# Ten warm products, no zero fill, and the first loads of q and k on one queue

## The chip, the cores and the metric

The kernel runs on one core of a Trainium2 chip. The metric is the device time of one execution in microseconds (us), the median of several. Before the change it is 364.73 us, the median of three runs from 364.7 to 364.95.

The engines that matter here: TensorE (PE in the profile; its weight loads are PEld), which multiplies and transposes; ScalarE (ACT) and VectorE (DVE), which work elementwise and move results out of PSUM; GpSimd (POOL), which here issues most of the loads; SyncE (SP), which issues DMAs. A DMA can be issued from the queues of SP, ACT and POOL.

## The reference

Attention with a squared relu in place of the softmax, and behind it a feed-forward block with the exact gelu:

```python
batch, n_heads, seq, head_dim = (8, 12, 448, 64)
scores = scale * np.matmul(q, k.transpose(0, 1, 3, 2))
attn = np.maximum(scores, 0.0) ** 2 / S
out = np.matmul(attn, v)
x = out.transpose(0, 2, 1, 3).reshape(B * S, H * D)      # 3584 x 768
h = x @ w_in                                             # 3584 x 2048
g = 0.5 * h * (1.0 + erf(h * inv_sqrt2))
return g @ w_out                                         # 3584 x 768
```

q, k, v and the weights come in float32; the products run in bf16.

## The kernel before

The twelve heads of a batch are taken in three groups of four. For a group, q and k are loaded with the rows of the sequence on the partitions and must be transposed, so that head_dim lies on the partitions. In batches 0 and 1 TensorE does that (`add_tq` and `add_tk`, tile `tp`, lines 676, 680, 708 and 715): a transpose is a product with an identity matrix, and a copy by DVE (line 566) brings the result from PSUM into `qT` and `kT`. From batch 2 on, DMA transposes issued by SP do it (line 742). The scores of 64 keys at a time go into PSUM (`ps`, line 819), ACT takes the relu of most of them (`a_sq`, line 831) and DVE of some (line 833), DVE squares them (line 841), and the products with v follow (`pav`, line 881). The feed-forward block is worked in between (`psh`, line 940), and later alone (lines 1092, 1281, 1388).

The order of the work of each engine is written out by hand in the string `ORDER`. A word is an engine's letter (P, A, D, G, S for PE, ACT, DVE, POOL, SP) and the number of an operation; a word with Z is a fill: products of zeros with that many columns in all, on TensorE (`add_fill`, line 1609). Each engine works through its words in order and waits at each one for what it reads and for the buffer that it writes. POOL's identity matrix (`make_ident`, line 1447) is the operation with the highest number; in `ORDER` it stands behind the first five loads that POOL issues.

Ahead of that list the kernel has a head of its own. The first group's first half of q (`q32`) and its k (`k32`) are loaded as float32, k in two parts: `K_CUT` = 4 blocks of 64 rows and then the remaining three. Then a tile of zeros and the identity's ground are set, a gelu on one column brings ACT's table in, and `SPIN` = 11 products of zeros with 512 columns run on TensorE:

```python
spin = banks.take("spin")
for _ in range(SPIN):
    wide = zero[:, :1].to_broadcast([128, NB])
    nc.tensor.matmul(spin[:, 0], zero, wide, start=True, stop=True)
```

The function `early` (line 1480) then casts what has landed: ACT casts q32 (word A10), DVE the first part of k32 (D13), ACT the second (A16). TensorE's first words are the transposes of this q (P11), of the first four blocks of k (P14) and of the other three (P17); DVE's next ones the copies into qT (D12) and kT (D15, D18). The transposes have two PSUM buffers, so P17 waits until D12 has freed one. P29 and P32 are the first scores. All other loads are issued by POOL, at most eight of them under way.

Of the kernel before, what the change touches and what calls it, by code (L numbers as in the profile page):

```python
# [84 lines left out]

COLD_END = 0.0
K_CUT = 4
SPIN = 11


ORDER = """
D13 G0 Z1056 A10 G1 G7 G4 A16 G108 G1469 P11 D12 P14 D15 P17 P29 P32 D18 P38 D39 P19 P21 A30 D20 P35
D22 P27 A33 P62 D31 P77 A36 D40 D28 A63 P59 D34 P44 P25 G2 G3 A78 A60 D37 D45 G111 P121 P65 A66 P71
A72 P47 P74 A75 D79 A48 D122 D64 D67 P23 D73 P50 D24 D26 P68 G107 P41 A51 P98 A69 D76 A99 D61 D52
D70 P53 P123 G5 G115 G112 A42 A43 G8 G116 A54 G6 P95 P86 A96 A87 P80 D46 D124 A81 A82 P89 P92 P119
# [339 lines left out]
def kernel(  # L435
# [9 lines left out]
    nc = tc.nc  # L445
# [25 lines left out]
    k32 = wpool.tile([128, 2, NK * D], F32, tag="t4", name="k32")  # L471
# [36 lines left out]
    def q_view(b, g0, g1, c0, c1):  # L508
        qq = q[b, 4 * g0 : 4 * g1].rearrange("h (p c) d -> p h (c d)", c=NC)
        return qq[:, :, c0 * D : c1 * D]  # L510
# [5 lines left out]
    def kv_view(t, b, g0, g1):  # L516

        return t[b, 4 * g0 : 4 * g1].rearrange("h s d -> (h s d)").rearrange(
            "(x p f) -> p x f", p=128, f=NK * D
        )  # L520
# [915 lines left out]


    first = slice(0, K_CUT * D)
    nc.scalar.dma_start(k32[:, :, first], kv_view(k, 0, 0, 1)[:, :, first])
    nc.sync.dma_start(q32, q_view(0, 0, 1, 0, HC))  # L1440
    rest = slice(K_CUT * D, NK * D)
    nc.scalar.dma_start(k32[:, :, rest], kv_view(k, 0, 0, 1)[:, :, rest])
    zero = const.tile([128, 128], BF16, tag="zero", name="zero")
    V.memset(zero, 0.0)
    V.memset(ident, 0.0)
# [12 lines left out]
# [3 lines that stand above are left out]
# [192 lines left out]
```

## Time and profile before

| what | us |
|---|---|
| median of the runs | 364.73 |
| the profiled execution | 364.86 |
| its span, first to last instruction | 363.1 |
| TensorE busy | 354.5 |
| DVE busy | 296.0 |
| ACT busy | 211.2 |
| POOL busy | 65.4 |

The span is what the profile sees between the first and the last instruction; the execution's time has 1.76 us more. Busy time is the union of an engine's instructions. Matmuls overlap and their ends are modelled, so a busy TensorE need not be at its peak. Times in the rows are in us from the start of the span: a row of the time line is start, duration, engine, line, operation, what is written and read, how many, and in brackets the idle time before it and what ended it. A "q" behind the engine's name is its queue, issuing a DMA. The chain of waits is the sequence of work that ended last, followed back from the last instruction. In answers by stretches a row has the stretch, its length, the busy time and count of PE, PEld, DVE, ACT and POOL, the granted clock of TensorE, the share of the DMA engines and the GB/s.

### The profile page before, as it was taken

What the parts mean: (1) busy time and instruction counts of PE and PEld (TensorE: products, weight loads), DVE (VectorE), ACT (ScalarE), POOL (GpSimd) and SP (SyncE); (2) the same over time, 40 slices, a digit from 0 to 9 for tenths busy, and PEclk for the clock granted to TensorE, in tenths of its full rate; (3) what the DMA queues carried; (4) which work ended last, traced back from release to release, by engine and by line L of the source; (5) the groups of instructions that cost most, each with busy time, mean ns of one, the idle gap of its engine ahead of it and who ended that gap; (6) DMA issues with size and microseconds to landing.
All of it is one profiled execution on the core that took longest, in us unless ns stands there. A gap on an engine that the chain in (4) does not pass through costs nothing.

```text
span 363.1 us, 7640 instructions
## 1 busy us (share of the span) xinstructions
PE 354.5 (98%) x3103; PEld 190.5 (52%) x3103; DVE 296.0 (82%) x497; ACT 211.2 (58%) x354; POOL 65.4 (18%) x102
## 2 busy tenths in 40 slices
PE   8799999999999999999999999999999999999995
PEld 3464544555554555554455555555555555555663
DVE  2999968869999979999979999998966655786552
ACT  3999766446678685777968864625741233662110
POOL 8566174110533051070000000000000000000000
PEclk9999999999999999999999999999999999999999
DMA  9999999999999999999950521000301210302223
GB/s 174 201 202 199 183 175 190 173 197 191 177 183 185 167 196 172 217 146 225 200 113 7 91 68 45 3 0 14 119 0 56 70 49 2 87 2 87 88 88 88
DMA packets 72083, 43.83 MB, mean 121 GB/s; under 512 B 36336, under 2 KB 68720, under 8 KB 72048
## 3 DMA queue, kind: packets, MB, share of 16 engines
q0 software_dynamic: 32032, 22.47, 43.9%
q1 hardware_dynamic: 39120, 20.03, 28.4%
q10 hardware_dynamic: 896, 0.85, 0.7%
q8 instruction: 24, 0.39, 0.5%
q14 instruction: 11, 0.09, 0.1%
HBM read 45.61 MB, written 11.01 MB: 156 GB/s over the span
## 4 chain that ended last, share of the span: by engine, by line
PE 94%; ACT 4%; issue 1%; DVE 1%
PE pso L1281 33%; PE psh L940 21%; PE pb L1092 18%; PE ps L819 9%; PE pav L881 8%; ACT a_sq L831 4%; PE pso L1388 3%; PE spin L1461 1%; ACT xT L568 0%; PE tp L715 0%; PE fill L1615 0%; DVE osb L1315 0%; DVE a_sq L841 0%; DVE qT L566 0%; PE tp L676 0%
## 5 line engine op out<-in xcount | busy, mean ns | idle before, releaser
L831 ACT ACTIVATE a_sq<-ps 128x896 bf16<-128x896 f32 x122 | 107.1, 923 | 29.4 <-PE ps L819 29.0
L841 DVE TENSOR_TENSOR a_sq<-a_sq 128x896 bf16<-128x896 bf16 x169 | 96.5, 614 | 2.0 <-ACT a_sq L831 1.6
L940 PE MATMUL psh<-xT,win_sb 128*128 128x448 bf16 x384 | 77.1, 353 | 0.0
L833 DVE TENSOR_SCALAR a_sq<-ps 128x896 bf16<-128x896 f32 (+1 forms) x47 | 50.5, 1076 | 14.1 <-PE ps L819 13.7
L1281 PEld LDWEIGHTS <-s_sb 128*128 128x128 bf16 x424 | 40.4, 98 | 29.7 <-issue 3.5
L940 PEld LDWEIGHTS <-win_sb 128*128 128x128 bf16 x384 | 35.6, 98 | 38.0 <-issue 7.1
L1123 DVE TENSOR_TENSOR part<-pb,part 128x448 f32<-128x448 f32 x80 | 46.4, 618 | 9.1 <-PE pb L1092 6.2
L819 PE MATMUL ps<-qT,kT 64*64 64x448 bf16 (+1 forms) x700 | 47.9, 350 | 2.2 <-ACT a_sq L831 2.0
L950 ACT ACTIVATE h_sb<-psh 128x448 bf16<-128x448 f32 x64 | 34.5, 548 | 19.0 <-PE psh L940 19.0
L1315 DVE TENSOR_TENSOR osb<-pso,p_sb 128x384 f32<-128x384 f32 x39 | 21.6, 553 | 23.7 <-PE pso L1281 18.2
L1281 PEld LDWEIGHTS <-h_sb 128*128 128x128 bf16 x296 | 28.2, 98 | 21.5 <-issue 3.0
L1281 PE MATMUL pso<-t_sb,s_sb 128*128 128x384 bf16 x208 | 38.1, 326 | 0.0
L1144 ACT ACTIVATE h_sb<-part 128x448 bf16<-128x448 f32 (+1 forms) x48 | 24.5, 537 | 22.8 <-DVE part L1123 22.7
L1281 PE MATMUL pso<-wout_sb,s_sb 128*128 128x384 bf16 (+1 forms) x208 | 37.7, 324 | 0.0
L881 PE MATMUL pav<-a_sq,v_sb 64*64 64x448 bf16 (+1 forms) x700 | 36.0, 342 | 0.8 <-ACT a_sq L831 0.8
L1281 PE MATMUL pso<-wout_sb,h_sb 128*128 128x384 bf16 x192 | 35.2, 326 | 0.0
L819 PEld LDWEIGHTS <-kT 64*64 64x64 bf16 x700 | 18.6, 105 | 25.1 <-issue 17.9
L1092 PEld LDWEIGHTS <-win_sb 128*128 128x128 bf16 x192 | 18.8, 98 | 16.7
L881 PEld LDWEIGHTS <-v_sb 64*64 64x64 bf16 x700 | 20.7, 107 | 12.4 <-issue 1.9
L1092 PE MATMUL pb<-xs,ws 128*128 128x448 bf16 x96 | 21.9, 352 | 0.0
L1092 PE MATMUL pb<-xs,win_sb 128*128 128x448 bf16 x96 | 21.8, 352 | 0.0
L1092 PE MATMUL pb<-xT,win_sb 128*128 128x448 bf16 x96 | 21.7, 352 | 0.0
(73 smaller groups left out, 310.5 us busy)
## 6 DMA issues: line engine op xcount, KB each, us to landing
nk<-in_k_dram POOLq DMA_DIRECT2D x23, 224.0 KB, 8.7
nq<-in_q_dram POOLq DMA_DIRECT2D x23, 224.0 KB, 8.8
v_sb<-in_v_dram POOLq DMA_DIRECT2D x4, 672.0 KB, 9.6
out_dram<-osb SPq DMA_DIRECT2D x7, 336.0 KB, 3.2
v_sb<-in_v_dram POOLq DMA_DIRECT2D x10, 224.0 KB, 8.0
out_dram<-osb SPq DMA_DIRECT2D x7, 288.0 KB, 3.4
out_dram<-osb SPq DMA_DIRECT2D x8, 240.0 KB, 2.8
win_sb<-in_moe_w_in_dram POOLq DMA_DIRECT2D x8, 192.0 KB, 9.4
```

The source lines that it names most:

```text
L819: nc.tensor.matmul(ps[64 * j : 64 * j + 64, e, x * w : x * w + w], kT[r, g, i * 128 + 64 * j : i * 128 + 64 * j + 64], moving, start=True, ...
L831: A.activation(ar, ps, AF.Relu, scale=c_att)
L833: V.tensor_scalar(ar, ps, c_att, 0.0, op0=mybir.AluOpType.mult, op1=mybir.AluOpType.max,)
L841: V.tensor_mul(box["a2"][:, :, :used], ar, ar)
L881: nc.tensor.matmul(pav[0][o2 : o2 + 64, e, :w], get_v()[r, 2 * v_slot(b, g) + e, bass.ts(i, D)], box["a2"][r, y, o : o + w], start=(i == 0 ...
L940: nc.tensor.matmul(ph[:, x * n : x * n + n], win_sb[:, kd, bass.ts(m + x, 128)], xT[b][:, kd, c], start=(kd == 0), stop=(kd == KD - 1),)
L950: A.activation(h_ring()[:, m : m + nm, o + c.start : o + c.stop], box[0][:, :S].rearrange("p (x n) -> p x n", x=nm), AF.Gelu,)
L1092: nc.tensor.matmul(ps[name][:, :S], w[:, k, bass.ts(mm, 128)], right()[:, k], start=first and k == 0, stop=k == K1 - 1, skip_group_check=n ...
L1123: V.tensor_add(get(to), ps[name][:, :S], get(other))
L1144: A.activation(to(), src()[:, n0:n1], AF.Gelu)
L1281: nc.tensor.matmul(box[bank][:, n0:n1], left()[:, kf], right()[:, kf, n0:n1], start=bool(need) and kf == 0, stop=kf == K2 - 1, skip_group_ ...
L1315: V.tensor_add(out()[:, n0:n1], box[bank][:, n0:n1], other()[:, n0:n1])
```

## The change

The constant `SPIN` falls from 11 to 10. The word Z1056, a fill of 1056 columns ahead of the first transposes, is taken out of `ORDER`; with it the fill's operation is gone, so the identity's number falls from 1469 to 1468 in the same place. The first three loads change their queues: before, the two of k32 were issued by ACT and the one of q32 by SP; now SP issues all three, q32 first, then the two parts of k32. Everything else stands in the same order.

```diff
 COLD_END = 0.0
 K_CUT = 4
-SPIN = 11
+SPIN = 10
...
 ORDER = """
-D13 G0 Z1056 A10 G1 G7 G4 A16 G108 G1469 P11 D12 P14 D15 P17 P29 P32 D18 P38 D39 P19 P21 A30 D20 P35
+D13 G0 A10 G1 G7 G4 A16 G108 G1468 P11 D12 P14 D15 P17 P29 P32 D18 P38 D39 P19 P21 A30 D20 P35
...
     first = slice(0, K_CUT * D)
-    nc.scalar.dma_start(k32[:, :, first], kv_view(k, 0, 0, 1)[:, :, first])
     nc.sync.dma_start(q32, q_view(0, 0, 1, 0, HC))
+    nc.sync.dma_start(k32[:, :, first], kv_view(k, 0, 0, 1)[:, :, first])
     rest = slice(K_CUT * D, NK * D)
-    nc.scalar.dma_start(k32[:, :, rest], kv_view(k, 0, 0, 1)[:, :, rest])
+    nc.sync.dma_start(k32[:, :, rest], kv_view(k, 0, 0, 1)[:, :, rest])
     zero = const.tile([128, 128], BF16, tag="zero", name="zero")
```

## The prediction

> **What bounds the kernel now.** I read the page first (span, shares of the chain), then the chain of waits in order of time, then the time line of the first 14 us engine by engine, then the DMA issues with their landings. The page:
>
> ```profile
> span 363.1 us, 7640 instructions
> ...
> PE 94%; ACT 4%; issue 1%; DVE 1%
> ```
>
> The chain of waits in order of time (start, us, what):
>
> ```profile
> 0.99 4.88 PE spin L1461 x11
> 5.87 0.80 PE fill L1615 x3
> ...
> 8.22 3.45 ACT a_sq L831 x4
> ...
> 34.01 2.38 PE psh L940 x12
> ```
>
> The answer by stretches, columns as on the page, ACT the fourth engine:
>
> ```profile
> 12.20:26.20 14.00, 11.93 (x280) 7.92 (x277) 13.77 (x25) 13.91 (x22) 8.62 (x13) 1.00 1.32 201
> ```
>
> TensorE is on the path almost to the end. Only the head differs: to 5.87 the path is eleven products on zeros, to 6.67 the zero fill, to 8.22 the first transposes and scores, and then ACT's relu (busy 13.91 of 14.00 us) until about 26, when TensorE takes over. The stretch on zeros computes nothing, so a microsecond cut from it arrives at the end, if whatever comes second allows. No DMA stands on this chain. What comes second is in the time line of the first 6 us:
>
> ```profile
> 0.74 0.47 ACTq L1439 DMA_DIRECT2D k<-in_k_dram  x1
> 0.74 0.38 SPq L1440 DMA_DIRECT2D q<-in_q_dram  x1
> ...
> 4.81 0.62 ACT L568 CAST nq<-q 112x512 bf16<-112x512 f32 x1 [1.55 <-DMA q<-in_q_dram]
> ...
> 4.96 0.34 POOL L1448 TENSOR_SCALAR_AFFINE_SELECT ident<-ident 128x128 bf16<-128x128 bf16 x1
> 5.07 0.52 DVE L566 CAST nk<-k 128x512 bf16<-128x512 f32 x1 [4.05 <-DMA k<-in_k_dram]
> ...
> 5.43 0.51 ACT L568 CAST nk<-k 128x384 bf16<-128x384 f32 x1
> ```
>
> And what follows, to the first scores:
>
> ```profile
> 6.60 0.37 PE L708 MATMUL tp<-ident,nq 112*128 112x112 bf16 x4
> ...
> 6.81 0.39 PE L676 MATMUL tp<-ident,nk 128*128 128x128 bf16 x4
> 7.01 0.39 DVE L566 COPY qT<-tp 128x448 bf16<-128x448 bf16 x1 [1.42 <-PE tp L708]
> 7.32 0.86 DVE L566 COPY kT<-tp 128x512 bf16<-128x512 bf16 x2
> ...
> 7.79 0.73 PE L819 MATMUL ps<-qT,kT 64*64 64x224 bf16 x20
> ```
>
> q is cast at 5.43 (4.81 + 0.62) and the identity is ready at 5.30 (4.96 + 0.34), yet the first transposes start at 6.60: TensorE itself is late by over 1.1 us.
>
> **The products taken away.** The last products on zeros, and the answers around the fill (start, us):
>
> ```profile
> 5.24 0.63 PE L1461 MATMUL spin<-zero 128*128 128x512 bf16 x1
> 5.80 0.63 PE L1615 MATMUL fill<-zero 64*64 64x512 bf16 x1
> 6.23 0.44 PE L1615 MATMUL fill<-zero 64*64 64x512 bf16 x2
> ```
>
> The eleventh product starts at 5.24; without it TensorE is free there. Without the fill nothing else stands before the transposes in its order. So they start when the latest of three things is there: TensorE at 5.24, the identity at 5.30, the cast of q. With the cast where it is, that is about 5.47 (0.04 behind the cast); with an earlier cast, about 5.35 (0.05 behind the identity, whose place behind five loads in POOL's queue isn't moved). The gain at this point is 6.60 - 5.47 = 1.13 to 6.60 - 5.35 = 1.25.
>
> **The loads moved.** The issues, with KB and us to landing, and one stretch of the loads:
>
> ```profile
> k<-in_k_dram ACTq DMA_DIRECT2D x1, 256.0 KB, 4.3
> q<-in_q_dram SPq DMA_DIRECT2D x1, 224.0 KB, 4.0
> 3.00:3.50 0.50, 0.50 (x2) 0.15 (x1) 0.00 (x0) 0.25 (x2) 0.50 (x2) 1.00 1.11 371
> ```
>
> Today q and the first part of k are issued together and share about 371 GB/s. With q in front, the k bytes that now move before q's last come after it: at most some 240 KB, or 0.65 us. So q lands between 0.65 us earlier and as now, and its cast ends between 4.8 and 5.4; either way the identity or the cast releases TensorE at 5.35 to 5.47. The first part of k is issued 0.38 us later, behind q's issue on SP, and waits for q's bytes; q and it together are the same 480 KB over the same engines, so it should still land near 5.04 (0.74 + 4.3). Its bounds: not earlier than 0.4 us before that, and at worst the issue's delay and all of q's exclusive time on top, 5.04 + 0.38 + 0.65 = 6.07. I take 5.07 for the start of its cast as now, since the rate is what this stretch is short of. The last part of k keeps the same bytes in front of it (cast from 5.43 to 5.94; its transposes wait for a PSUM buffer that the qT copy frees at 5.76 + 0.39 = 6.15 by the sum below, so 0.2 us to spare). ACT loses two issues ahead of its table load and its warm-up, which have no reader before the first relu's; SP has nothing else until 32 us. Both cost nothing.
>
> **Down to the first relu.** Transposes of q at 5.35; the qT copy starts 0.41 behind them as now (7.01 - 6.60), at 5.76, when DVE has cast k (5.07 + 0.52 = 5.59). The k transposes can start at 5.62, behind that cast, and end at 6.01 (0.39); the kT copy follows the qT copy 0.31 later as now, at 6.07. So k's landing has 0.06 us to spare; each tenth that it is later than that costs a tenth. Scores at 7.79 - 1.25 = 6.54, first relu at 8.22 - 1.25 = 6.97.
>
> **Through the stage bounded by ACT.** All of it moves up alike as long as its loads are there; POOL's loads don't move, since their queue and bytes are as before. The two tightest, issue, landing and first reader of each (the second is the load of the third batch's k):
>
> ```profile
> 2.06 2.85 POOL L514 DMA_DIRECT2D nq<-in_q_dram  x4
> nq<-in_q_dram POOLq DMA_DIRECT2D x1, 224.0 KB, 5.4
> 8.45 0.58 PE L680 MATMUL tp<-ident,nk 128*64 128x128 bf16 x14
> 8.86 0.56 PE L715 MATMUL tp<-ident,nq 112*64 112x112 bf16 x16
> 40.75 1.23 SPq L742 DMA_TRANSPOSE kT<-nk  x1
> kT<-nk SPq DMA_TRANSPOSE x1, 7.9
> 49.90 0.38 PE L819 MATMUL ps<-qT,kT 64*64 64x448 bf16 x4
> ```
>
> The first lands at 7.5 and is read at 8.86: 1.4 us to spare. The transposed k of batch 2 lands at 48.65 and is read at 49.90: 1.25 to spare. A gain of 1.25 just fits; more wouldn't.
>
> **The sum.** 0.43 for the eleventh product (5.24 to 5.67 in its spacing), 0.80 for the fill, less 0.03 to 0.1 of waiting for the identity or the cast: 1.13 to 1.25, and I take 1.2 less 0.05 for the two margins that it uses up: 1.15. The profiled execution took 364.86 (1.76 outside its span, unchanged), so it becomes 363.71; it is 0.13 above the median of the runs, 364.73, from which the sum gives 363.58. I forecast 363.6.
>
> **The clock: the rival on the other side.** The zeros also run TensorE up. A spin product of 512 columns takes 0.63 and they follow each other by 0.43; the fill's second product and a small third are through in 0.44 together. At full speed twelve of 448 columns take 2.38, or 0.20 each. So the clock doubled at about 6.2 to 6.3, some 5.3 us after the first product; the granted clock of the page says 1.00 there and doesn't show it, the durations do. The change ends the unbroken work at 5.44 instead of after 6.67, followed by bursts with pauses for casts and copies. If the step comes at 6.3 all the same, only the first transposes run slowly: four spacings of 0.05 doubled, twice, some 0.3 us, 363.9, inside the forecast's own range. If the pauses put it off, the price grows: to the first relu about 0.45 (transposes and eight scores doubled), and then the rows from 8.23 to 9.75 (0.58, 0.56 and eight scores) doubled, 1.0 more, in a place where the third relu starts 0.07 behind its scores and so has no cover. With the step after about 9 the gain is used up: 364.9. With the step past 11, another 0.5 or more: 365.5, slower than before. For it: 4.45 us unbroken, where this execution shows 5.3 until the step. Against: after 1.9 or so us of pure work nothing says that pauses of 0.2 us count as rest, and the stage from 12 to 26, with TensorE busy 11.93 of 14.00, keeps its full clock.
>
> The Trainium skill, "TensorE: Matmul & The Clock Gate", Part 1, speaks against the change here: the full clock is granted at the end of a free-running window of about 3.4 us in which TensorE was busy. The step at 6.2 to 6.3 fits it (it allows 4.4 to 7.8 for a start at 0.99). By that rule strictly read, an estimate from its figure, a whole window fits into 4.45 us in about 3 executions of 10 and into the present 5.7 in 7 of 10, and the rest would fall to the cases of 364.9 and later; no row here says how full the window must be.
>
> **The other rivals.** k late: if one queue in a row serves k 0.4 to 1.0 us later than two side by side, the kT copy waits and 0.4 to 0.9 of gain is left; 364.2 at the middle. For it: the later issue (0.38) and only 0.06 of cover. Against: the bytes and the rate are the same. The head is hidden anyway: if a POOL load lands 0.5 to 1 us later or a margin is smaller than it looks, ACT or TensorE waits at 8 or 50 us and gives most of it back; 364.6. Against: the chain has no DMA in it, and the two rows above are the tightest that I found.
>
> **How the numbers follow.** Forecast 363.6 (own range 363.2 to 364.0): 0.64. k late, 364.2: 0.12. Clock late but before about 11, 364.9: 0.10. Clock later than that, 365.5: 0.07. Margins give it back, 364.6: 0.07. About 0.2%, 0.73 us, is what can be told from no change: faster is the forecast and a little of the late k, 0.66; slower is the last clock case, 0.07; the same is the rest, 0.27. The range runs from 363.1 (1.6 saved, if the clock also steps earlier) to 364.9.
>
> **What would show it.** Right: transposes of q at 5.35 to 5.47 with q's cast ended before, kT copy near 6.07, first relu near 7.0, all later rows some 1.15 earlier up to the last store. k late: DVE's cast of nk starts after 5.2 and the kT copy follows it. Clock: score products of 224 columns that take over 0.3 after 7 us, and ACT idle before its third relu. Margins: TensorE waiting for a DMA at 7.5 or at 48.6. Wrong altogether: a first relu at 7.0 and an end as before.

## The result, and the profile after

The change makes the kernel slower: 368.65 us, the median of five executions from 367.18 to 369.36, against 364.73 for the kernel before, a ratio of 1.0106 with a 95% interval of 1.0091 to 1.0122. Forecast were 363.6, in a range of 363.1 to 364.9. The profiled execution took 368.91 us, 4.05 more than that of before. The page of the kernel after:

```profile
span 367.1 us, 7632 instructions
...
PEclk9799999999999999999999999999999999999999
...
PE 89%; ACT 3%; DVE 3%; DMA 2%; issue 1%; SPq 0%; DVEq 0%
```

Two things are new: a DMA stands on the chain that ended last (2%), and the granted clock of TensorE has a 7 in the second slice, where before every slice had a 9. The chain of waits of the kernel after, in order of time (start, us, what):

```profile
1.18 0.48 SPq L1440
...
1.70 7.04 DMA k<-in_k_dram
...
8.75 0.52 ACT nk L568
...
9.32 0.50 PE tp L676 x3
```

The path no longer starts with the products on zeros. It starts with three issues in a row on SP's queue and waits 7.04 us for the last of them, the last part of k. The time lines of TensorE, ACT and DVE of the kernel after:

```profile
5.35 0.36 PE L708 MATMUL tp<-ident,nq 112*128 112x112 bf16 x4 [0.50 <-POOL ident L1448]
...
9.32 0.50 PE L676 MATMUL tp<-ident,nk 128*128 128x128 bf16 x3 [3.39 <-ACT nk L568]
...
10.83 0.96 PE L680 MATMUL tp<-ident,nk 128*64 128x128 bf16 x14
11.57 0.96 PE L715 MATMUL tp<-ident,nq 112*64 112x112 bf16 x16
...
3.45 0.62 ACT L568 CAST nq<-q 112x512 bf16<-112x512 f32 x1 [1.22 <-DMA q<-in_q_dram]
8.75 0.51 ACT L568 CAST nk<-k 128x384 bf16<-128x384 f32 x1 [4.68 <-DMA k<-in_k_dram]
10.39 1.73 ACT L831 ACTIVATE a_sq<-ps 128x896 bf16<-128x896 f32 x2 [1.13 <-PE ps L819]
...
4.21 0.43 DVE L566 CAST nk<-k 128x512 bf16<-128x512 f32 x1 [3.19 <-DMA k<-in_k_dram]
...
6.05 0.42 DVE L566 COPY kT<-tp 128x512 bf16<-128x512 bf16 x1
```

To 6.05 everything is as forecast or better: the transposes of q start at 5.35 and the kT copy at 6.05. Then TensorE stands idle for 3.39 us, until the cast of k's last part. The first relu starts at 10.39 instead of 8.22, and the transposes behind it take 0.96 where the same numbers of them took 0.58 and 0.56.

That third transfer among the DMA issues of the kernel after (KB, us to landing):

```profile
k<-in_k_dram SPq DMA_DIRECT2D x1, 192.0 KB, 7.0
```

and its answer by stretches (stretch, length, then PE, PEld, DVE, ACT, POOL, clock, DMA share, GB/s):

```profile
2.00:2.50 0.50, 0.50 (x3) 0.15 (x1) 0.00 (x0) 0.22 (x2) 0.50 (x2) 1.00 0.91 271
...
3.50:4.00 0.50, 0.50 (x3) 0.20 (x2) 0.00 (x0) 0.50 (x1) 0.50 (x1) 1.00 1.00 140
4.00:4.50 0.50, 0.50 (x4) 0.23 (x3) 0.29 (x1) 0.07 (x1) 0.50 (x2) 1.00 0.84 102
...
7.00:8.00 1.00, 0.00 (x0) 0.00 (x0) 0.00 (x0) 0.00 (x0) 0.35 (x1) 0.76 1.52 177
8.00:9.00 1.00, 0.00 (x0) 0.00 (x0) 0.00 (x0) 0.25 (x1) 0.18 (x1) 0.50 1.51 192
...
14.00:15.00 1.00, 0.66 (x12) 0.28 (x5) 1.00 (x4) 0.88 (x3) 0.63 (x1) 0.82 1.27 203
```

The same two views of the kernel before, first the issue:

```profile
k<-in_k_dram ACTq DMA_DIRECT2D x1, 192.0 KB, 4.2
```

then the stretches:

```profile
2.00:2.50 0.50, 0.50 (x3) 0.15 (x1) 0.00 (x0) 0.50 (x1) 0.50 (x2) 1.00 0.64 40
...
4.00:4.50 0.50, 0.50 (x3) 0.22 (x2) 0.00 (x0) 0.00 (x0) 0.50 (x2) 1.00 1.15 319
```

The same 192 KB took 4.2 us on ACT's queue and 7.0 as the third transfer on SP's. After the change the DMA engines start earlier (271 GB/s at 2.0 to 2.5 against 40), but between 3.5 and 4.5 they fall to 140 and 102 GB/s, where the kernel before still moved 319 from 4.0 to 4.5. And the clock: 0.76 in the stretch from 7 to 8 is full speed to 7.52 and half from there (0.52 + 0.48 x 0.5), 0.82 in the one from 14 to 15 is half speed to 14.36. So TensorE's clock stood at half for 6.8 us; TensorE waited for the first 1.8 of them and worked at half speed from 9.32 on, through the first scores.

How much later (+) or earlier than in the kernel before each kernel of this study is, in its profiled execution; the columns are the first relu, the first product with v (16.77 us before), two later products with v (105.4 and 124.1 before) and the end of the span (363.06):

```
                          relu    16.8   105.4   124.1     end
after                    +2.17   +3.39   +3.40   +3.39   +4.08
products and fill only   -0.69   -0.69   -0.69   -0.30   -0.30
loads only               +0.86   +1.99   +2.00   +1.99   +2.17
last part of k on ACT    -0.97   -1.03   -1.02   -0.31   -0.27
the same, again          -1.13   -1.19   -1.19   +0.01   -0.31
the same, third time     -1.02   -0.77   -0.76   -0.39   -0.50
zeros in the gap         +1.94   +2.02   +2.02   +2.02   +3.07
POOL's loads, first try  +1.43   +3.80   +3.80   +3.80   +3.76
POOL's loads late        -1.87   +2.57   +2.60   +3.01   +2.64
all gates as DMAs        -0.98   -0.92   -0.72   -0.73   +2.80
one gate as a DMA        -1.13   -0.04   +2.92   +2.92   +3.12
before, gates as DMAs    +0.21   +0.22   +0.22   +0.22   +0.27
```

Of the +4.08 of the kernel after, 2.17 are there at the first relu, 1.22 more by the first product with v, and 0.69 come later (0.6 of it between 168 and 179 us, where TensorE waits for DVE; what DVE lost there is told below).

### The profile page after: what moved, and what is told of

It reads as the page before. It is cut to its first block, busy times and chain, and to the rows that moved or that the text cites. A ratio compares the mean times of both kernels' runs of the same rounds, so it can differ in the third digit from the quotient of the medians.

```text
span 367.1 us, 7632 instructions
## 1 busy us (share of the span) xinstructions
PE 354.7 (97%) x3099; PEld 191.2 (52%) x3099; DVE 296.4 (81%) x497; ACT 211.4 (58%) x354; POOL 64.7 (18%) x102
## 4 chain that ended last, share of the span: by engine, by line
PE 89%; ACT 3%; DVE 3%; DMA 2%; issue 1%; SPq 0%; DVEq 0%
PE pso L1281 32%; PE psh L940 20%; PE pb L1092 17%; PE ps L819 9%; PE pav L881 7%; PE pso L1388 3%; ACT a_sq L831 3%; DMA k<-in_k_dram 2%; DVE a_sq L841 1%; DVE osb L1315 1%; PE tp L715 1%; DVE qT L566 0%; ACT xT L568 0%; DVE a_sq L833 0%; PE tp L680 0%
## 5 line engine op out<-in xcount | busy, mean ns | idle before, releaser
L819 PE MATMUL ps<-qT,kT 64*64 64x448 bf16 (+1 forms) x700 | 48.8, 358 | 2.1 <-ACT a_sq L831 1.9
```

Of the source, the lines that this page charges most:

```text
L819: nc.tensor.matmul(ps[64 * j : 64 * j + 64, e, x * w : x * w + w], kT[r, g, i * 128 + 64 * j : i * 128 + 64 * j + 64], moving, start=True, ...
```

## The experiments

**The two halves of the change.** First, the products and the fill alone, with the three loads on their old queues:

```diff
-SPIN = 11
+SPIN = 10
-D13 G0 Z1056 A10 G1 G7 G4 A16 G108 G1469 P11 ...
+D13 G0 A10 G1 G7 G4 A16 G108 G1468 P11 ...
```

> Ten products and no zero fill, with the three loads on their old queues. If the loss comes from the last part of k landing late (the load theory), nothing is late here: first transposes at 5.35 to 5.47, first relu near 7.0, no drop of the granted clock, 363.6 us. If the loss comes from the missing products on zeros (the clock theory), TensorE runs slowly after its zeros as before: score products of 224 columns over 0.3 us until 11 or later, first relu at 7.5, 366 us or more.

Measured: 364.61 us, ratio 0.9996 (0.9987 to 1.0005). Its time lines of TensorE and ACT:

```profile
5.91 0.37 PE L708 MATMUL tp<-ident,nq 112*128 112x112 bf16 x4 [1.23 <-ACT nq L568]
...
5.23 0.62 ACT L568 CAST nq<-q 112x512 bf16<-112x512 f32 x1 [1.97 <-DMA q<-in_q_dram]
```

The transposes start 0.69 earlier than before (6.60), and not 1.13: TensorE now waits 1.23 us for the cast of q, which landed at 5.21 here, 0.42 later than in the kernel before, although its issue is the same; why is open. So without the new order of the loads q is the limit, and with it (5.35 in the kernel after) the identity is. No clock is lost, but the first relu comes at 7.53, not near 7.0, and the time that the load theory expected, 363.6, isn't reached: most of the gain is gone at the end (the table), which is followed below.

Then the loads alone, with eleven products and the fill:

```diff
-    nc.scalar.dma_start(k32[:, :, first], ...)
     nc.sync.dma_start(q32, ...)
+    nc.sync.dma_start(k32[:, :, first], ...)
-    nc.scalar.dma_start(k32[:, :, rest], ...)
+    nc.sync.dma_start(k32[:, :, rest], ...)
```

> Eleven products and the fill as before; only the three loads stand in a row on SyncE's queue. Load theory: q lands near 3.4, the first part of k near 4.2, the last part near 8.7; the transposes of the last part start after 9.3 and the first relu comes near 10.4; the products hide nothing of it: 367 to 369 us. Clock theory: the loads cost nothing behind 6.7 us of work on zeros: 364.5 to 365.

Measured: 367.86, four executions from 367.05 to 372.34, ratio 1.0115 (1.007 to 1.016). TensorE's time line:

```profile
8.37 0.34 PE L676 MATMUL tp<-ident,nk 128*128 128x128 bf16 x3 [1.40 <-ACT nk L568]
...
9.43 0.96 PE L680 MATMUL tp<-ident,nk 128*64 128x128 bf16 x14
```

The whole loss sits in the loads: the last part of k landed at 7.78 here, and the transposes behind it run at half speed (0.96) as in the kernel after. The ratios of the halves, 0.9996 and 1.0115, give 1.0111 together; the change measured 1.0106, within the interval of the second half.

**The third load off SP's queue.** The changed kernel, with only the last part of k back on ACT's queue:

```diff
-    nc.sync.dma_start(k32[:, :, rest], ...)
+    nc.scalar.dma_start(k32[:, :, rest], ...)
```

> The changed kernel, but the last part of k is issued by ScalarE, as its first instruction, instead of third on SyncE's queue. Load theory: it lands by 5.5, nothing waits for it, 363.5 us. If it is not the queue but the early end of the first two loads that lets POOL's loads in, the last part lands late here too and the time stays over 366. Clock theory: 366 or more either way.

Measured: 364.4, ratio 0.9995 (0.9984 to 1.0007). The last part of k, issued at 0.74, landed at 4.6, q at 4.4, the first part of k at 5.2; the transposes start at 5.36 and the first relu at 7.25. So one line of the change carries the loss. What this run doesn't tell: whether the queue or the time of the issue matters, since ACT issues it at 0.74 and SP at 1.70. Two more runs were to separate these, by an issue on ACT's queue placed behind ACT's table load:

> The changed kernel, but ScalarE issues the last part of k, behind its table load and warm-up, at about 2.1 us: later than SyncE did (1.70), but on a queue of its own. If the late landing comes from standing third in SyncE's queue, it lands by 5.5 here, and the time is 364.4 as with the load at ScalarE's head. If it comes from starting when POOL's loads start (3.3 us), it lands after 7 here too, TensorE waits for it, and the time is 366.5 or more.

> The changed kernel, but the last part of k is issued by ACT behind its table load and its warm-up, at about 2.2 us, half a microsecond later than SP issued it in the changed kernel (1.70). Theory A (its place as the third transfer on SP's queue is what holds it): on a queue of its own it has no q and no first part of k in front of it and lands 4 to 5 us after its issue, by 6.7 at the latest; TensorE waits for it about 1 us instead of 3.4, and the time is 364.5 to 366. Theory B (what holds it is that it starts no earlier than POOL's loads, whatever its queue): it lands at 8.3 or later, since it starts even later than in the changed kernel, the first relu comes at 10 or later, and the time is 367.5 to 369, as the changed kernel's.

Both missed their aim: the profile shows the issue at 0.74 again, ahead of the table load, the first time where it was written behind the identity's function, the second time as an operation of its own at the head of the list.

```profile
0.74 0.47 ACTq L1623 DMA_DIRECT2D k<-in_k_dram  x1
1.24 1.28 ACT L1455 ACT_TABLE_LOAD   x1 [1.24 <-PEq L1640]
```

So they repeat the run above: 364.45, ratio 1.0002 (0.9991 to 1.0013), and 364.11, ratio 0.9988 (0.9976 to 0.9999). An issue on ACT's queue at 1.7 us wasn't tried.

**Does the third load meet POOL's loads?** POOL's first load is issued at 1.24 in both kernels; in the kernel before its first bytes move at 4.28, in the kernel after at 3.29, while the last part of k is under way. A first try to delay it, by four fills of an unused tile:

> The changed kernel, all three loads in a row on SyncE's queue, but POOL writes a scratch tile four times (some 1 us) before its first load, so that its loads start later by that. If the last part of k is late because POOL's loads meet it, it lands near 5 here, the transposes and the first relu come near 7.0, and the time is 364 to 365 (POOL's own loads are later by 1 us and may then be waited for). If it is late by its place in the queue alone, it lands near 8.5 as in the change and the time stays over 367.

It missed its aim: only one fill came ahead of POOL's first load, which was still issued at 1.27; the others fell between the loads. The time was 368.14, ratio 1.0104 (1.0089 to 1.0119), and the rate fell to 157 and 73 GB/s between 3.5 and 4.5 as in the kernel after. The second try puts the identity and nine such fills into POOL's list ahead of its loads:

```diff
-D13 G0 A10 G1 G7 G4 A16 G108 G1468 P11 ...
+G1468 G1469 D13 G0 A10 G1 G7 G4 A16 G108 P11 ...
+    def hold(e):
+        for _ in range(9):
+            nc.gpsimd.memset(held, 0.0)
+    sch.add((("POOL", 2.8, 2.9),), hold)
```

> The changed kernel, but POOL makes the identity first and then writes 9 unused tiles of 128x256 before it issues its first load, so that this load is issued near 4 us instead of 1.24 and its packets start near 6. The three loads on SP's queue then have the DMA engines to themselves until then. Theory B (the last part of k is held because it meets POOL's loads): it lands between 5 and 6 us, the rate of the DMA engines stays over 300 GB/s to its end, and the first relu comes before 7.5. Theory A (the third place on one queue is slow by itself): it lands at 8 or later with the engines mostly idle. The time of the whole says less, since all of POOL's loads come 2.7 us late and the transposes of the second and third group wait for them: 365 to 369 by both.

Measured: 368.48, ratio 1.0102 (1.0082 to 1.0122). The time lines of POOL, ACT and TensorE:

```profile
4.52 0.82 POOL L605 DMA_DIRECT2D nk<-in_k_dram  x1
...
5.07 0.51 ACT L568 CAST nk<-k 128x384 bf16<-128x384 f32 x1 [0.69 <-DMA k<-in_k_dram]
6.35 1.73 ACT L831 ACTIVATE a_sq<-ps 128x896 bf16<-128x896 f32 x2 [0.77 <-PE ps L819]
...
8.65 0.58 PE L680 MATMUL tp<-ident,nk 128*64 128x128 bf16 x14 [1.93 <-DMA nk<-in_k_dram]
```

The third transfer among its DMA issues:

```profile
k<-in_k_dram SPq DMA_DIRECT2D x1, 192.0 KB, 3.3
```

Its answer by stretches:

```profile
3.00:3.50 0.50, 0.50 (x2) 0.15 (x1) 0.00 (x0) 0.00 (x0) 0.41 (x2) 1.00 1.07 331
3.50:4.00 0.50, 0.50 (x3) 0.25 (x2) 0.00 (x0) 0.23 (x1) 0.42 (x2) 1.00 1.06 315
```

With POOL's load issued at 4.52, the same third transfer on the same queue, issued at the same 1.70, takes 3.3 us instead of 7.0 and lands at 5.05; the rate holds at 331 and 315 GB/s, and the first relu is at 6.35. Theory A (the third place on one queue is slow by itself) falls; theory B stands: what holds the last part of k is that POOL's loads run beside it. Whether it is their bytes or POOL's work of issuing them isn't separated, since both are moved. The early relu is owed in part to the identity, which this kernel also makes earlier (its first transposes start at 4.47). The whole gains nothing by it, as expected, since the loads held back are then late themselves: TensorE waits 1.93 us for one until 8.65, and 0.77 for another until 10.00. It loses its clock here too: 0.74 in the stretch from 10 to 11 and 0.50 in the next.

**The price of the clock.** The changed kernel with a fill of 7168 columns of zeros in the gap, ahead of the three transposes that wait for k's last part:

```diff
-... P11 D12 P14 D15 P17 ...
+... P11 D12 P14 D15 Z7168 P17 ...
```

> The changed kernel with products of zeros, 7168 columns in all (some 3.1 us at full clock), put between the transposes of the first and of the last part of k, where TensorE waited. The last part of k still lands near 8.7. Load theory: the wait stays but the clock stays up: first relu near 10.2, the stage behind it at full speed, 366.3 to 367, so that of the loss of 3.9 about half is the wait by itself and the rest its second price, the clock. Clock theory: the whole loss goes, 364.7 or less.

Measured: 368.31, ratio 1.0104 (1.0081 to 1.0128). TensorE's time line:

```profile
6.32 3.20 PE L1615 MATMUL fill<-zero 64*64 64x512 bf16 x14 [0.26 <-DVE qT L566]
9.45 0.34 PE L676 MATMUL tp<-ident,nk 128*128 128x128 bf16 x3
...
10.46 0.58 PE L680 MATMUL tp<-ident,nk 128*64 128x128 bf16 x14
```

and one stretch:

```profile
11.00:12.00 1.00, 0.96 (x34) 0.74 (x28) 1.00 (x3) 1.00 (x3) 0.65 (x1) 1.00 1.32 203
```

The last part of k is as late (landed at 8.50), but the clock stays at 1.00 and the transposes take 0.58. The delay at the first product with v is +2.02 instead of +3.39, so the half clock costs about 1.4 us there, and more of the loss of 3.39 is the wait by itself. The first relu came at 10.16, as expected (10.2), the time not (366.3 to 367). To 124 us the difference stays; then this kernel waited for a DMA transpose of k (issued at 116.1, landed at 128.6) and lost 1.03 more, so that its median is only 0.34 below that of the kernel after. Why that transpose was late here wasn't followed further.

**Where the gain at the head goes.** With the third load on ACT's queue, 1.0 to 1.1 us are won at the first relu and 0.8 to 1.2 are there at 105 us, but only 0.3 to 0.5 at the end. The chain of the first of these runs around that place:

```profile
94.11 8.16 DMA nk<-in_k_dram
...
102.29 11.71 DMA kT<-nk
```

and its time line of POOL:

```profile
90.05 3.29 POOL L787 COPY gate<-qT 128x16 bf16<-128x16 bf16 x1 [13.07 <-DMA qT<-nq]
93.28 0.84 POOL L623 DMA_DIRECT2D v_sb<-in_v_dram  x1
...
97.48 0.71 POOL L605 DMA_DIRECT2D nk<-in_k_dram  x1
98.18 1.42 POOL L514 DMA_DIRECT2D nq<-in_q_dram  x2
```

In the kernel before the same copy, which only makes POOL wait until qT is there, took:

```profile
90.24 0.44 POOL L787 COPY gate<-qT 128x16 bf16<-128x16 bf16 x1 [12.78 <-DMA qT<-nq]
90.76 0.84 POOL L623 DMA_DIRECT2D v_sb<-in_v_dram  x1
```

A copy of 128x16 takes 3.29 us instead of 0.44, the loads behind it are issued 2.5 us later, and three more POOL loads are issued at 97 to 99, just ahead of SP's transpose of k at 102.29; it then takes 11.71 us and lands at 114.00, where TensorE waits. The copy was long in all four kernels of this study that were ahead there and still had it (3.54, 3.29, 3.63 and 3.79 us), but also in the kernel with POOL's loads late, which was 2.6 behind (3.20).

The gain is lost in two steps. In all four, 0.4 goes before the product with v at 113.05, where TensorE waits for DVE near 106.5; the late transpose takes 0.3 and 0.8 more in two of them, the first two runs with the load on ACT, and nothing in the other two. What DVE lost stands in its time line, in the run above:

```profile
98.61 1.22 DVE L566 COPY qT<-qT 64x896 bf16<-64x896 bf16 x2
```

and in the kernel before:

```profile
99.63 0.79 DVE L566 COPY qT<-qT 64x896 bf16<-64x896 bf16 x2
```

The same two copies take 0.43 us longer, beside the three loads that POOL issues from 97.48 to 99.60. In the five kernels that lose 0.4 there (these four and the one with POOL's loads late) they take 1.20 to 1.23 us, in the eight others 0.79. The 0.6 that the kernel after loses between 168 and 179 us has the same look: its two copies from 164.97 take 1.48 us beside POOL's loads, against 0.92 in the kernel before. This is read from the traces; no run changed the copies themselves.

While POOL's copy was long, DVE ran instructions with two inputs back to back, in the run above six of them from 89.50 to 93.27, of which four begin after the copy:

```profile
89.50 1.15 DVE L841 TENSOR_TENSOR a_sq<-a_sq 128x896 bf16<-128x896 bf16 x2
...
92.58 0.69 DVE L1260 TENSOR_TENSOR s_sb<-s_sb,h_sb 128x1024 bf16<-128x1024 bf16 x1
```

The Trainium skill, "SBUF — State Buffer", section "Who interferes with whom", says that a DVE instruction with two inputs in SBUF contends with a GpSimd instruction that reads SBUF, and that such contention is an exclusive lock on a shared pair of ports. The trace agrees as far as the copy ends with the last of these instructions (93.34 and 93.27); that it was blocked through several of them in a row, the page doesn't say. Nor do such rows alone decide it: in the kernel before DVE ran the same kind of instructions back to back from 89.66 to 94.35, and the copy at 90.24 took 0.44. What lets POOL in there stays open.

To test whether the long copy gives the gain back, the copies were replaced, so that POOL no longer reads SBUF itself, both times in the kernel with the third load on ACT's queue: all fifteen by small DMAs, then only the first of batch 3.

```diff
-            nc.gpsimd.tensor_copy(gate, q_seg(...)[:, : SEG : SEG // 16])
+            nc.gpsimd.dma_start(gate, q_seg(...)[:, :16])
```

> The kernel with the last part of k at ScalarE's head, and POOL's gates (line 787), which copied 16 columns of qT only to wait for its landing, made into small DMAs with the same wait. Theory of the gain that is lost: the gate at 90 us took 3.3 us behind VectorE there (0.4 before), put three of POOL's loads ahead of SyncE's transposes, and the k of a batch landed at 114.0, where TensorE took the 1.0 us back. Then the gates here take under 1 us, TensorE's 12th product with v stays 1.0 earlier than before the change, and the time is 363.7. If the loss at 105 to 124 us is the bandwidth of the DMA engines itself, it comes back at the same place whatever POOL's order, and the time is 364.4.

> The kernel with the last part of k on ACT's queue, with one more edit: the first gate of batch 3, a copy of 128x16 on POOL that took 3.3 us at 90 us there, is a small DMA on POOL's queue; the other fourteen gates stay copies. Theory (this one long copy is what gives the gain back at 114 us): POOL's loads behind it are issued at 91 again as before the change, TensorE doesn't wait for the transposed k at 114, the 0.7 to 1.2 us gained at the head last beyond 124 us and the time is 363.5 to 364.0, ratio 0.997 to 0.999. Rival (another late transfer or another long copy behind it takes its place): the gain is gone by 200 us again and the time is 364.3 to 364.6, or has single executions of 367 and more, as with all gates as DMAs.

Measured, all gates: 364.44, ratio 1.0013 (0.9989 to 1.0037), with ten executions from 363.2 to 365.54 and two of 367.64 and 368.02. One gate: 364.3, ratio 0.9995 (0.9976 to 1.0013), ten from 363.33 to 365.2 and two of 367.32 and 367.97. The profile caught one of the long executions both times. In both the place at 105 to 124 us is passed without loss: the first keeps its gain (-0.72 at 105, -0.73 at 124) to 163 us, the second its delay (+2.92 at both).

The second run missed its aim, though. The copy at that place is still a copy, and still long; the small DMA stands two gates behind it, at 100.43:

```profile
94.87 2.41 POOL L791 COPY gate<-qT 128x16 bf16<-128x16 bf16 x1 [13.08 <-DMA qT<-nq]
```

So the long copy alone is not enough to cost the 0.4 or to make the transpose late. With the one gate as a DMA the three loads no longer follow each other there, and DVE's two copies take 0.79 again. The run with all gates, where no copy is long and the two DVE copies take 0.79 too, fits the same account: what costs is where POOL's later loads fall. That is argued from two executions that differ in much else; no run moved these loads alone.

Other losses came instead: in the first run, 3.3 us at 184 to 198, where TensorE waits for a DMA transpose of k; in the second, 4.1 us between the first relu and 74 us. The first 1.1 of these fall where a load that POOL issued at 5.91 landed at 15.25 and TensorE waited for it; behind it the granted clock drops (0.78 from 15 to 16, 0.50 from 16 to 17); the rest wasn't followed. The same gates in the kernel before:

> The kernel before, with only the gates made into small DMAs: the control of the run with the gates and the load at ScalarE's head. Either theory: nothing waits for these gates in the kernel before, 364.7 within 0.3; what the other run is faster than this one is the head's gain as it arrives at the end.

364.51, ratio 1.0026 (0.9999 to 1.0052), again with three executions near 368.2 among twelve, which the plain kernel before didn't show in 29. So the gate DMAs bring such executions by themselves. What makes them long stays open.

## Why the prediction was wrong

**Ten products, no fill: right.** The transposes of q were forecast at 5.35 and started at 5.35, behind the identity (idle until POOL's ident). The kT copy was forecast at 6.07 and started at 6.05.

**q and the first part of k: right in what follows, wrong in size.** q was to land at most 0.65 earlier than its 4.79; it landed at 3.43, and the first part of k at 4.18 instead of 5.04. The bound took the bytes moved at a fixed rate, but the rate had a slow start of its own: 40 GB/s at 2.0 to 2.5 with ACT and SP issuing at once, 271 with SP alone.

**The last part of k: this step failed.** "The last part of k keeps the same bytes in front of it (cast from 5.43 to 5.94; ..." and "POOL's loads don't move, since their queue and bytes are as before". The cast began at 8.75. The bytes in front of it are the same on paper, but it is issued at 1.70 instead of 1.24 and it shares its time with POOL's loads, whose bytes began to move at 3.29 instead of 4.28. It was given 0.2 us to spare, and I priced lateness only for the first part of k, which came early. The rival "k late" had the right kind of wait, the wrong part, and at 0.4 to 1.0 us less than a third of its size: forecast first relu 6.97, measured 10.39, 3.42 later. With POOL's loads out of the way the last part of k would have been in time (landed at 5.05, before the 5.41 of the kernel before).

The Trainium skill, "DMA: Bandwidth & Descriptors", section "Issuing engines are not separate DMA queues", says that transfers of all issuing engines run on the same 16 DMA engines and interleave, and that issuing from several engines saves only the time of issuing. The first half is what the runs show. By the second half the move to one queue would cost the 0.46 us of the later issue; it cost 3.3 us of landing time here (8.73 against 5.41), and with POOL's loads held back nothing (5.05), so that the rest of the price comes from what the transfer interleaved with.

**The clock: right in kind, as a second price.** I gave 0.17 to a clock that is late. It wasn't late: the products on zeros took 0.38 us instead of 0.63 from 4.25 on. In the ten kernels of this study with ten products the step to full clock came between 3.7 and 6.2 us by the durations of their products and transposes, in the three with eleven and the fill between 5.9 and 6.8, so that the 6.2 to 6.3 on which I built was one draw; with the pauses it came no later in any of them than without. But the gap of 3.39 us took it away again at 7.52, and the price was about 1.4 us at the first product with v, by the run with zeros in the gap. The Trainium skill, "TensorE: Matmul & The Clock Gate", Part 1, has the clock decided over free-running windows of about 3.4 us. The rows agree: half speed from 7.52 to 14.36 is 6.84, two such windows. The strict reading in the prediction, that TensorE must work through a whole window first, isn't borne out: the step came 3.1 us after the first product in the kernel after, and 2.7 after it with POOL's loads late. My argument against this rival was that pauses of 0.2 us need not count as rest; none of the runs lost its clock over such pauses. A longer pause did it, as in the run with the loads alone:

```profile
6.00:7.00 1.00, 0.98 (x11) 0.53 (x9) 0.21 (x1) 0.00 (x0) 1.00 (x2) 1.00 1.30 188
7.00:8.00 1.00, 0.00 (x0) 0.00 (x0) 0.51 (x2) 0.19 (x1) 0.46 (x2) 1.00 1.56 181
8.00:9.00 1.00, 0.63 (x19) 0.51 (x19) 0.25 (x1) 0.32 (x1) 0.63 (x2) 1.00 1.53 191
9.00:10.00 1.00, 1.00 (x28) 0.68 (x18) 0.56 (x2) 0.92 (x2) 1.00 (x2) 0.64 1.46 197
```

0.64 puts the fall at 9.28. In the 3.42 us before it TensorE had a pause of 1.40 and was busy for about 2.0 (0.13 + 0.98 + 0.63 + 0.28), or 59%, and lost the clock all the same. With the products alone it had a pause of 1.23, was busy for 1.92 of the 3.41 us from 3.75 on, and kept it. So the busy share doesn't decide it by itself; what does stays open.

**The margins: right in kind, mostly in the wrong place.** I named the load of the second group's q (read at 8.86 before) and the kT of batch 2 at 49.90. The first did bound one of the kernels with the third load on ACT: its transposes start at 8.22, 0.27 behind the transposes before them, waiting for that DMA, and its gain goes from -1.02 to -0.77. The second was passed. But the gain went at 105 to 114, in a wait for DVE and, in two kernels, for a late kT, which no margin of loads in the kernel before shows: its kT for that place was there 8 us early. So even without the late k the forecast would have been 0.5 to 0.9 us too good: 364.1 to 364.45 in three measurements, where the sum gives 363.58; that term, the head's gain taken to the end, was mis-sized too (0.3 to 0.5 in place of 1.15).

## What to carry to other kernels

A load is not only its bytes and its rate: ask which other queues start to move while it is under way, and give every part of a transfer that is split its own landing time and its own margin. A stall near the start has a second price, when the gap is long enough to lose TensorE's clock; the table of granted clock by stretches shows both. And a microsecond won at the head is won only when the last margin behind it holds: measure the delay at several places along the kernel, and look there, in each engine's rows, where it changes.

## What the runs showed of the hardware

When the first loads were issued from ACT and SP at the same moment, little moved at first (40 to 99 GB/s at 2.0 to 2.5 us in eight traces); three loads in a row from SP moved 183 to 271 GB/s there (five traces). POOL's first bytes also came later in the first case, at 4.0 to 4.3 us against 3.3 to 3.5 (in the four of the five where they weren't held back). Why is open. When POOL's casting loads and the tail of SP's transfers met, the sum of both fell to 102 GB/s in the kernel after, less than either had alone (315 to 331 for SP's, 203 for POOL's at 14 to 15 us). A copy of 128x16 on GpSimd took up to 3.79 us beside DVE's instructions with two inputs, and two DVE copies of 64x896 that take 0.79 us took up to 1.48 beside loads that POOL issued.
